# A cross network's last unit: second recursion level inside two products, one more addition on TensorE, and output blocks that leave by other queues and in halves

## The chip, the cores and the metric

The kernel runs on one core of a Trainium2 chip. The metric is device time in microseconds (us), the median of a few executions on one chip, lower is better. The experiments ran on several chips, each beside the kernel before on the same chip; its median in those rounds was 2277.26 to 2277.31 us. The profile is one execution; its span is some 2 us shorter than the time of the same execution. All runs quoted as timed were in the undisturbed state, with a granted TensorE clock of 0.998 to 1.0. The one exception is a run that was looked at once only, whose state is unknown; it is named where it comes up.

Most times below are counted from the first product matmul of the last unit, which I call **F**. "Tail" means F to the end of the span. A "run" is an experiment; where a store is said to have 512 "runs", these are its contiguous pieces in memory.

## The reference, cut to what matters

```python
B, D, L = 16384, 1024, 6            # bf16
x = x0
for l in range(L):
    proj = x @ ws[l] + bs[l]
    x = x0 * proj + x
return x
```

## The kernel before

The batch is cut in 16 blocks of 1024 rows; each goes through 6 layers, which makes 96 **units**. A unit is one 1024 x 1024 x 1024 product by Strassen-Winograd: seven half-size products P1 to P7 instead of eight. In most units products 5 and 2 are split the same way a second time: 56 matmuls of 256 columns in place of 32 of 512. x is kept transposed (features on partitions), so the last unit must turn its result round before it is stored.

Every operation has a rank, and operations are put into the engines' programs in rank order as their inputs are ready. The last unit has ranks of its own (`RLAST`). It is single-level here, as all units of the first row block are:

```python
units = [(pr, l) for pr in range(NPAIR) for l in range(L)]
NU = len(units)
level1 = lambda u: units[u][0] == 0 or u == NU - 1
...
        for m in range(KH):
            group(f"P1.{m}", "1", pA[m], A[m], B11, [XI[0, 0]], m, True)
            if one:                       # 16 matmuls of 512 columns for each of P2 and P5
                copy(f"F1.{m}", pX[m][:], pA[m][:], [A[m]], [Xn[m]])
                group(f"P2.{m}", "2", pX[m], Xn[m], B21, [XI[1, 0], Xn[m]], m, False)
                biased(f"E2.{m}", Q[:, m, :], pX[m][:], 0, m, [Xn[m]], [f"Q.{m}"])
                group(f"P5.{m}", "5", pX[m], Xn[m], T[1], ["T1"], m, True)
                copy(f"E5.{m}", P5s[:, m, :], pX[m][:], [Xn[m]], [f"5c.{m}"])
            ...                           # else: seven inner products, 28 matmuls of 256 each
```

The output has four blocks: Q ("11"), U ("12"), V ("22") and W ("21"). Q and U are turned by a DMA transpose and then stored; V and W are turned by TensorE into PSUM (the accumulator memory), copied out as bf16 ("cast"), and stored. W's residual x is added by TensorE (`xW`, x transposed into the same bank); V's by VectorE (`Vx`).

```python
            for h in range(2):
                sl = slice(h * KQ, (h + 1) * KQ)
                for nm, C, q in (("U", U, (0, 1)), ("V", V, (1, 1))):
                    ...                                            # Ua, Um, Va, Vm: add P5, times x0
                ttop(f"Vx{h}", V[:, sl], V[:, sl], blk(xs, 1, 1)[:, sl], ADD, ...)
                ttop(f"Ux{h}", ...)
            for m in range(KH):
                ttop(f"Wm{m}", W[:, m, :], W[:, m, :], blk(x0T, 1, 0)[:, m, :], MULT, ...)
            for nm, n in (("Q", 0), ("U", 1)):
                def tr(n=n, xfin=xfin, xo=xo):
                    nc.sync.dma_start_transpose(out=xo[:, 0, n]..., in_=xfin[:, 0, n]...)
                add("tr" + nm, tr, ...)
                def st(n=n, xo=xo, r0=r0):
                    nc.sync.dma_start(out[r0 + n * NB:r0 + (n + 1) * NB, 0:H]..., xo[:, 0, n]...)
                add("st" + nm, st, [f"xo{nm}"], ["out"])
            ...                                                    # tV, xW, tW, casts, stVa, stVb, stWa, stWb
```

By rank SyncE's program is: transpose Q, transpose U, store Q, store U, then V's two halves and W's first; W's second half goes by ScalarE's queue.

Of the kernel before, what the change touches and what calls it, by code (L numbers as in the profile page):

```python
# [9 lines left out]
ADD = mybir.AluOpType.add  # L10
SUB = mybir.AluOpType.subtract
MULT = mybir.AluOpType.mult
# [5 lines left out]
def ranks(text):  # L18

    return {w.split("@")[0]: float(w.split("@")[1]) for w in text.split()}  # L20
# [106 lines left out]
T1@-1.18 5t13@.65 5t2@3.13 2t13@3.47 5t4@5.20 2t2@6.67 T2@7.01 2t4@8.14 T3@8.48 T4@9.61 2cc@12.46 Q1@13.20 Qm@14.47  # L127
5cc@15.61 Qa@16.21 Ua@17.45 Um@18.72 Ux@19.99 Va@21.12 Wma@23.49 Wmb@24.69 Wx@25.43 Vm@27.50 Vx@28.97
""")]
RLAST = {**R0, **ranks("""  # L130
P6.0@10.4 P6.1@11.3 P6.2@12.1 P6.3@13 P3.0@13.9 P3.1@14.7 P3.2@15.6 P3.3@16.4 P7.0@17.3 P7.1@18.2 P7.2@19 P7.3@19.9
P4.0@20.8 P4.1@21.6 P4.2@22.5 P4.3@23.3
P2.0@3.5 P2.1@4.4 P2.2@5.2 P2.3@6.1 P5.0@6.9 P5.1@7.8 P5.2@8.7 P5.3@9.5 tV.0@24.4 tV.1@24.6 tV.2@24.8 tV.3@25
xW.0@25.1 tW.0@25.2 xW.1@25.3 tW.1@25.4 xW.2@25.5 tW.2@25.6 xW.3@25.7 tW.3@26.6
F1.0@2.8 F1.1@3.2 F1.2@3.7 F1.3@4.1 E2.0@4.6 E2.1@5.4 E2.2@6.3 E2.3@7.2 E5.0@8.3 E5.1@9.2 E5.2@10 E5.3@10.9 F.0@11.5 F.1@12.3 F.2@13.2 F.3@14.1 E3.0@15 E3.1@15.8 E3.2@16.7 E3.3@17.5 E7.0@18.4 E7.1@19.3 E7.2@20.1 E7.3@21
E4.0@21.9 E4.1@22.7 E4.2@23.6 E4.3@24.4 cV.0@25 cV.1@25.1 cV.2@25.2 cV.3@25.3 cW.3@27
T4@12 Qm@12.5 Qa@13.6
Ua0@16.6 Um0@17.2 Ux0@17.8 Ua1@18.4 Um1@19 Ux1@19.6 Va0@20.4 Vm0@21 Vx0@21.3 Va1@21.6 Vm1@22.2 Vx1@22.8
Wm0@22.9 Wm1@23.7 Wm2@24.6 Wm3@25.4 cW.0@26.3 cW.1@26.5 cW.2@26.7
trQ@19 stQ@24 trU@22.5 stU@26 stVa@27 stVb@27.5 stWa@28 stWb@29  # L140
""")}
SPAN2, SPAN0 = 23.4, 24.2

# [2 lines left out]
def kernel(  # L146
# [7 lines left out]
    nc = tc.nc  # L154
    P = nc.NUM_PARTITIONS
    B, D = x0.shape
    L = ws.shape[0]
    KD = D // P
    KH = KD // 2
    H = D // 2  # L160
    NB = 512
# [3 lines left out]
    KQ, HQ, NQ = KH // 2, H // 2, NB // 2  # L165
# [12 lines left out]
    pA = [psum.tile([P, NB], FP32, name=f"pA{i}") for i in range(KH)]  # L178
    pX = [psum.tile([P, NB], FP32, name=f"pX{i}") for i in range(KH)]
    x0Ts = [work.tile([P, 2, KD, NB], BF16, name=f"x0T{i}") for i in range(2)]  # L180
    xsts = [work.tile([P, 2, KD, NB], BF16, name=f"xst{i}") for i in range(2)]
# [4 lines left out]
    P1s, P5s, Q, U, V, W = (work.tile([P, KH, NB], BF16, name=f"ev{i}") for i in range(6))  # L186
# [5 lines left out]
    b_all = const.tile([P, LK], FP32, name="b_all")  # L192

    def blk(t, dh, n):
        return t[:, n, dh * KH:(dh + 1) * KH, :]
# [12 lines left out]

    units = [(pr, l) for pr in range(NPAIR) for l in range(L)]
    NU = len(units)  # L210
    level1 = lambda u: units[u][0] == 0 or u == NU - 1
    RAW = [("4", "load"), ("w12", "stage"), ("1", "load"), ("2", "load")]
    MAKE = [(w, "make") for w in ("5", "6", "7", "3")]
    ring_seq = [(0, w, k) for w, k in RAW]
    for u, (pr, l) in enumerate(units):
        if pr == 0:
            ring_seq += [(u + 1, w, k) for w, k in RAW if l < L - 1] + [(u, w, k) for w, k in MAKE]
        else:
            order = "1 2 5 6 7 3 4" if level1(u) else "1 5 5i 2 2i 6 3 7 4"
            ring_seq += [(u, w, "load") for w in order.split()]  # L220
    wt, uses_left, live = {}, {}, []
    pos = {"next": 0}

# [43 lines left out]
    for u, (pr, l) in enumerate(units):  # L267
# [8 lines left out]
        def add(name, fn, rd=(), wr=(), weights=(), rk=rk, base=base, u=u):  # L276
            op(base + rk[name], fn, rd, wr, [(u, w) for w in weights])

        def ttop(name, o, a, b, o_, rd, wr, **kw):
            add(name, lambda: tt(o, a, b, o_), rd, wr, **kw)  # L280
# [11 lines left out]
        def biased(name, dst, src, eh, m, rd, wr, l=l):  # L292
            c = l * KD + eh * KH + m
            add(name, lambda: nc.scalar.activation(out=dst, in_=src, func=IDENT, bias=b_all[:, c:c + 1], scale=1.0), rd, wr)  # L294
# [114 lines left out]
                     ip5[X][:].unsqueeze(1).to_broadcast([P, 2, KQ, NQ]), ADD, [X + "u0", X + "u1", X + "ps"],  # L409
                     cn(0, 1) + cn(1, 1))  # L410
        for m in range(KH):
            xb = m if one else m % 2
            group(f"P6.{m}", "6", pA[m], A[m], T[2], ["T2", A[m]], m, False)
            copy(f"F.{m}", pX[xb][:], pA[m][:], [A[m]], [Xn[xb]])
            group(f"P3.{m}", "3", pX[xb], Xn[xb], B22, [XI[1, 1], Xn[xb]], m, False)
            biased(f"E3.{m}", U[:, m, :], pX[xb][:], 0, m, [Xn[xb]], [f"U.{m}"])
            group(f"P7.{m}", "7", pA[m], A[m], T[3], ["T3", A[m]], m, False)
            biased(f"E7.{m}", V[:, m, :], pA[m][:], 1, m, [A[m]], [f"V.{m}"])
            group(f"P4.{m}", "4", pA[m], A[m], T[4], ["T4", A[m]], m, False)
            biased(f"E4.{m}", W[:, m, :], pA[m][:], 1, m, [A[m]], [f"W.{m}"])  # L420
        allm = lambda s: [f"{s}.{m}" for m in range(KH)]
        if not one:
            ttop("Q1", Q[:], Q[:], P1s[:], ADD, allm("Q") + allm("P1s"), allm("Q"))
# [11 lines left out]
        else:  # L435
# [2 lines left out]
            quad = lambda t: t[:].rearrange("r n k (j p) -> r (n k j) p", p=P).rearrange(  # L438
                "r (e n j k) p -> r e n j k p", e=2, n=2, j=KH)
            xfin, xo = quad(xsts[free]), quad(x0Ts[free])  # L440
            XF = [f"xs.{free}.{a}{b}" for a, b in QD]
            XT = [f"x0.{free}.{a}{b}" for a, b in QD]
            r0 = pr * PR
# [5 lines left out]
# [3 lines that stand above are left out]
                    ms = half(nm, h)  # L452
                    ttop(f"{nm}a{h}", C[:, sl], C[:, sl], P5s[:, sl], ADD, ms + half("5c", h), ms)
                    ttop(f"{nm}m{h}", C[:, sl], C[:, sl], blk(x0T, *q)[:, sl], MULT, ms + [X0[q]], ms)
                ttop(f"Vx{h}", V[:, sl], V[:, sl], blk(xs, 1, 1)[:, sl], ADD, half("V", h) + [XI[1, 1]], half("V", h))
                ttop(f"Ux{h}", xfin[:, 0, 1].rearrange("r j k p -> r k j p")[:, sl], v4(U[:])[:, sl],
                     v4(blk(xs, 0, 1))[:, sl], ADD, half("U", h) + [XI[0, 1]] + XF, [f"xfU{h}"])
            for m in range(KH):
                ttop(f"Wm{m}", W[:, m, :], W[:, m, :], blk(x0T, 1, 0)[:, m, :], MULT, [f"W.{m}", X0[1, 0]], [f"W.{m}"])
            for nm, n in (("Q", 0), ("U", 1)):  # L460
                def tr(n=n, xfin=xfin, xo=xo):
                    nc.sync.dma_start_transpose(out=xo[:, 0, n].rearrange("p j k r -> p (j k) r"),
                                                in_=xfin[:, 0, n].rearrange("r j k p -> r (j k p)"))
                add("tr" + nm, tr, [f"xf{nm}0", f"xf{nm}1"] + XT, [f"xo{nm}"])

                def st(n=n, xo=xo, r0=r0):
                    nc.sync.dma_start(out[r0 + n * NB:r0 + (n + 1) * NB, 0:H].rearrange("(j p) d -> p j d", p=P),
                                      xo[:, 0, n].rearrange("p j k r -> p j (k r)"))
                add("st" + nm, st, [f"xo{nm}"], ["out"])
            for nm, C, bank, n in (("V", V, pX, 1), ("W", W, pA, 0)):  # L470
                for m in range(KH):
                    bn = (Xn if nm == "V" else A)[m]

                    def part(src, start, stop, bank=bank, m=m):
                        for j in range(KH):
                            nc.tensor.matmul(bank[m][:, j * P:(j + 1) * P], lhsT=src[:, m, j * P:(j + 1) * P], rhs=ident[:],
                                             start=(start and j == 0), stop=stop, skip_group_check=True)
                    if nm == "W":
                        add(f"xW.{m}", lambda part=part, xs=xs: part(blk(xs, 1, 0), True, False), [XI[1, 0]], [bn])
                    add(f"t{nm}.{m}", lambda part=part, C=C, nm=nm: part(C, nm == "V", True), [f"{nm}.{m}", bn], [bn])  # L480

                    def cp(bank=bank, m=m, n=n, nm=nm, xo=xo):
                        d, s_ = xo[:, 1, n][:, :, m, :], bank[m][:].rearrange("p (j r) -> p j r", r=P)
                        if nm == "V" or m == 3:
                            nc.scalar.copy(out=d, in_=s_)
                        else:
                            nc.vector.tensor_copy(out=d, in_=s_)  # L487
                    add(f"c{nm}.{m}", cp, [bn] + XT, [f"xo{nm}.{m}"])

                def st2(k0, k1, eng=nc.sync, n=n, xo=xo, r0=r0):  # L490
                    eng.dma_start(out[r0 + n * NB:r0 + (n + 1) * NB, H + k0 * P:H + k1 * P].rearrange("(j p) d -> p j d", p=P),
                                      xo[:, 1, n][:, :, k0:k1].rearrange("p j k r -> p j (k r)"))
                add(f"st{nm}a", lambda st2=st2: st2(0, KQ), half(f"xo{nm}", 0), ["out"])
                add(f"st{nm}b", lambda st2=st2, nm=nm: st2(KQ, KH, nc.sync if nm == "V" else nc.scalar), half(f"xo{nm}", 1), ["out"])
# [118 lines left out]
```

## Time and profile before

| what | value | from |
|---|---|---|
| time | 2277.72 us | median of three runs (2276.81 to 2277.87) |
| span of the profiled execution, clock | 2275.2 us, 0.999 | profile |
| F to the end of product 4 on TensorE | 24.17 us | timeline of TensorE |
| F to the end of the last cast | 27.91 us | timelines of VectorE and ScalarE |
| F to the last landing of a store | 31.75 us | landings in the trace |
| F to the end of the span (tail) | 33.07 us | 2275.24 - 2242.17 |

The lines of the profile are shown in the prediction. The tail has two chains: compute (up to the last cast at 27.91) and the 16 shared DMA engines (full for the 9.5 us from 21.8 to 31.3).

### The profile page before, as it was taken

The numbers are of one execution on the slowest core, as the hardware profiler recorded it, in microseconds if no ns is written. First come the engines' busy times: TensorE is split into PE (matmuls) and PEld (weight loads), VectorE is DVE, ScalarE is ACT, GpSimd is POOL, SyncE is SP. The second block draws the span as 40 slices with busy tenths as digits, with TensorE's granted clock in tenths as the row PEclk, the third lists the DMA queues.
The fourth block names the chain that finished last, engine by engine and source line by source line (L and its number), as shares of the span: only waits on it lengthen the run. The fifth ranks groups of instructions, "written<-read, shape, count | busy, mean of one in ns | idle before, by whom it ended". The sixth has DMA issues, their size and how long they took to land.

```text
span 2275.2 us, 34978 instructions
## 1 busy us (share of the span) xinstructions
PE 2265.4 (100%) x12951; PEld 1264.0 (56%) x12951; DVE 2079.9 (91%) x2326; ACT 1839.4 (81%) x3228; POOL 22.1 (1%) x43
## 2 busy tenths in 40 slices
PE   9999999999999999999999999999999999999998
PEld 4455555555555555555555555555555555555554
DVE  7999999999999999999999999999999999999997
ACT  5678888888888888888888888888888888888887
POOL 1110000000000000000000000000000000000000
PEclk9999999999999999999999999999999999999999
DMA  9779797796977969779697796978969689696872
GB/s 279 229 270 289 261 242 269 219 301 209 252 257 221 288 217 260 250 226 283 213 274 241 228 283 204 273 245 230 283 200 292 226 232 286 194 303 216 241 240 65
DMA packets 625868, 557.01 MB, mean 245 GB/s; under 512 B 397600, under 2 KB 552224, under 8 KB 625696
## 3 DMA queue, kind: packets, MB, share of 16 engines
q1 hardware_dynamic: 618864, 534.58, 79.1%
q0 software_dynamic: 5184, 18.88, 2.2%
q8 instruction: 101, 1.65, 0.3%
q10 hardware_dynamic: 1648, 1.32, 0.2%
q14 instruction: 71, 0.58, 0.1%
HBM read 436.22 MB, written 52.43 MB: 215 GB/s over the span
## 4 chain that ended last, share of the span: by engine, by line
PE 98%; DVE 1%; SPq 0%; DMA 0%; issue 0%; ACT 0%; DVEq 0%
PE pA L285 57%; PE pX L389 24%; PE pX L285 16%; DVE ev L198 1%; SPq L529 0%; DMA wp<-in_ws_dram 0%; DVE xst L198 0%; DVE T L198 0%; DVE ti L198 0%; DVE wp L198 0%; SPq L538 0%; ACT ev L294 0%; DVE x0T L487 0%; DVEq L608 0%; DVEq L198 0%
## 5 line engine op out<-in xcount | busy, mean ns | idle before, releaser
L285 PEld LDWEIGHTS <-wp 128*128 128x128 bf16 x7904 | 772.3, 98 | 843.7 <-issue 3.9
L285 PE MATMUL pA<-T,wp 128*128 128x512 bf16 x4608 | 1054.9, 379 | 0.5 <-DVE T L198 0.5
L294 ACT ACTIVATE ev<-pA,b_all 128x512 bf16<-128x512 f32 x1124 | 704.8, 690 | 211.8 <-PE pA L285 211.4
L389 PEld LDWEIGHTS <-wp 128*128 128x128 bf16 x4984 | 487.1, 98 | 156.6 <-issue 15.2
L198 DVE TENSOR_TENSOR ev<-ev,x0T 128x2048 bf16<-128x2048 bf16 (+2 forms) x484 | 482.7, 999 | 8.1 <-ACT ev L294 1.5
L198 DVE TENSOR_TENSOR xst<-ev,xst 128x2048 bf16<-128x2048 bf16 x319 | 388.9, 1219 | 18.6 <-DVE ev L198 0.5
L389 PE MATMUL pX<-ti,wp 128*128 128x256 bf16 x2848 | 397.6, 272 | 0.0
L198 DVE TENSOR_TENSOR ev<-ev,ev 128x2048 bf16<-128x2048 bf16 (+1 forms) x283 | 343.7, 1215 | 26.7 <-ACT ev L294 9.8
L294 ACT ACTIVATE ev<-pX,b_all 128x512 bf16<-128x512 f32 x412 | 289.4, 705 | 59.9 <-PE pX L285 49.3
L285 PE MATMUL pX<-xst,wp 128*128 128x512 bf16 x1376 | 336.4, 379 | 0.0
L285 PE MATMUL pA<-xst,wp 128*128 128x512 bf16 x1280 | 313.5, 379 | 0.0
L290 ACT COPY pX<-pA 128x512 f32<-128x512 f32 x412 | 256.3, 625 | 44.7 <-PE pA L285 44.3
L290 ACT CAST ev<-pX 128x512 bf16<-128x512 f32 x384 | 224.8, 619 | 49.0 <-ACT ev L294 37.6
L198 DVE TENSOR_TENSOR ev<-iu,ip 128x1024 bf16<-128x1024 bf16 x178 | 122.4, 688 | 120.7 <-ACT iu L290 120.7
L290 ACT COPY pX<-pX 128x512 f32<-128x512 f32 x356 | 208.7, 587 | 8.4
L290 ACT CAST iu<-pX 128x512 bf16<-128x512 f32 x356 | 196.8, 639 | 0.0
L198 DVE TENSOR_TENSOR T<-xst 128x2048 bf16<-128x2048 bf16 x160 | 194.8, 1217 | 0.3
L198 DVE TENSOR_TENSOR T<-xst,T 128x2048 bf16<-128x2048 bf16 x160 | 194.5, 1216 | 0.0
L389 PE MATMUL pX<-T,wp 128*128 128x256 bf16 x1068 | 160.2, 273 | 0.0
L290 ACT CAST ip<-pX 128x512 bf16<-128x512 f32 x178 | 104.7, 589 | 54.1 <-PE pX L389 54.1
L389 PE MATMUL pX<-xst,wp 128*128 128x256 bf16 x888 | 133.2, 273 | 0.0
L198 DVE TENSOR_TENSOR xst<-ev,x0T 128x2048 bf16<-128x2048 bf16 x64 | 78.2, 1222 | 1.6
(44 smaller groups left out, 624.3 us busy)
## 6 DMA issues: line engine op xcount, KB each, us to landing
wp<-Lc SPq DMA_DIRECT2D x538, 512.0 KB, 4.6
wp<-in_ws_dram SPq DMA_DIRECT2D x285, 512.0 KB, 5.3
out_dram<-x0T SPq DMA_DIRECT2D x30, 1024.0 KB, 8.6
Lc<-wp POOLq DMA_DIRECT2D x24, 512.0 KB, 6.2
Lc<-isum POOLq DMA_DIRECT2D x12, 512.0 KB, 6.9
w<-in_ws_dram SPq DMA_DIRECT2D x5, 512.0 KB, 6.3
wp<-in_ws_dram ACTq DMA_DIRECT2D x2, 512.0 KB, 5.8
out_dram<-x0T SPq DMA_DIRECT2D x2, 512.0 KB, 3.6
```

Of the source, the lines that this page charges most:

```text
L198: nc.vector.tensor_tensor(out=o, in0=a, in1=b, op=op)
L285: nc.tensor.matmul(bank[:], lhsT=wt[(u, w)][:, k, m * P:(m + 1) * P], rhs=rhs[:, k, :], start=(start and k == 0), stop=(k == KH - 1), skip ...
L290: add(name, lambda: nc.scalar.copy(out=dst, in_=src), rd, wr)
L294: add(name, lambda: nc.scalar.activation(out=dst, in_=src, func=IDENT, bias=b_all[:, c:c + 1], scale=1.0), rd, wr)
L389: nc.tensor.matmul(pX[bank][:, m * NQ:(m + 1) * NQ], lhsT=wv[:, k, m * P:(m + 1) * P], rhs=rhs[:, k, :], start=(start and m == 0 and k == ...
```

## The change

Its intent is to save TensorE 0.74 us by the second level, to take work from VectorE (the addition of x to V, and one bias-add that is fused with a multiply), and to let Q and U leave before V and W need the DMA engines. The core of the diff (the new ranks, and access patterns, are cut):

```diff
-level1 = lambda u: units[u][0] == 0 or u == NU - 1
+level1 = lambda u: units[u][0] == 0
...
-                biased(f"E4.{m}", W[:, m, :], pA[m][:], 1, m, [A[m]], [f"W.{m}"])
+            if not (last and m == KH - 1):
+                biased(f"E4.{m}", W[:, m, :], pA[m][:], 1, m, [A[m]], [f"W.{m}"])
...
-                ttop(f"Vx{h}", V[:, sl], V[:, sl], blk(xs, 1, 1)[:, sl], ADD, ...)
...
-            for m in range(KH):
+            for m in range(KH - 1):
                 ttop(f"Wm{m}", ...)
+            add("Wm3", lambda c=c, x0T=x0T: nc.vector.scalar_tensor_tensor(
+                out=W[:, KH - 1, :], in0=pA[KH - 1][:], scalar=b_all[:, c:c + 1],
+                in1=blk(x0T, 1, 0)[:, KH - 1, :], op0=ADD, op1=MULT), ...)
+            outs = [("Q", xfin[:, 0, 0], xo[:, 0, 0], 0, 0, H)]
+            outs += [(f"U{h}", xfU[:, h], xoU[:, h], NB, h * HQ, (h + 1) * HQ) for h in range(2)]
+            for nm, src, dst, r, c0, c1 in outs:
+                add("tr" + nm, lambda src=src, dst=dst: nc.sync.dma_start_transpose(...), ...)
+                add("st" + nm, lambda ...: nc.gpsimd.dma_start(out[r:r + NB, c0:c1]..., dst...), ...)
...
-                    if nm == "W":
-                        add(f"xW.{m}", ...)
+                    add(f"x{nm}.{m}", lambda part=part, xs=xs, n=n: part(blk(xs, 1, n), True, False), [XI[1, n]], [bn])
...
-                        if nm == "V" or m == 3:
+                        if nm == "V" or m in (0, 2):      # which casts ScalarE does
```

More of the change, by code (lines that the diff above doesn't have):

```diff
@@ L129 @@
 """)]
-RLAST = {**R0, **ranks("""
-P6.0@10.4 P6.1@11.3 P6.2@12.1 P6.3@13 P3.0@13.9 P3.1@14.7 P3.2@15.6 P3.3@16.4 P7.0@17.3 P7.1@18.2 P7.2@19 P7.3@19.9
-P4.0@20.8 P4.1@21.6 P4.2@22.5 P4.3@23.3
-P2.0@3.5 P2.1@4.4 P2.2@5.2 P2.3@6.1 P5.0@6.9 P5.1@7.8 P5.2@8.7 P5.3@9.5 tV.0@24.4 tV.1@24.6 tV.2@24.8 tV.3@25
-xW.0@25.1 tW.0@25.2 xW.1@25.3 tW.1@25.4 xW.2@25.5 tW.2@25.6 xW.3@25.7 tW.3@26.6
-F1.0@2.8 F1.1@3.2 F1.2@3.7 F1.3@4.1 E2.0@4.6 E2.1@5.4 E2.2@6.3 E2.3@7.2 E5.0@8.3 E5.1@9.2 E5.2@10 E5.3@10.9 F.0@11.5 F.1@12.3 F.2@13.2 F.3@14.1 E3.0@15 E3.1@15.8 E3.2@16.7 E3.3@17.5 E7.0@18.4 E7.1@19.3 E7.2@20.1 E7.3@21
-E4.0@21.9 E4.1@22.7 E4.2@23.6 E4.3@24.4 cV.0@25 cV.1@25.1 cV.2@25.2 cV.3@25.3 cW.3@27
-T4@12 Qm@12.5 Qa@13.6
-Ua0@16.6 Um0@17.2 Ux0@17.8 Ua1@18.4 Um1@19 Ux1@19.6 Va0@20.4 Vm0@21 Vx0@21.3 Va1@21.6 Vm1@22.2 Vx1@22.8
-Wm0@22.9 Wm1@23.7 Wm2@24.6 Wm3@25.4 cW.0@26.3 cW.1@26.5 cW.2@26.7
-trQ@19 stQ@24 trU@22.5 stU@26 stVa@27 stVb@27.5 stWa@28 stWb@29
+RLAST = {**R2, **ranks("""
+xV.0@24.3 tV.0@24.4 xV.1@24.5 tV.1@24.6 xV.2@24.7 tV.2@24.8 xV.3@24.9 tV.3@25 xW.0@25.1 tW.0@25.2 xW.1@25.3 tW.1@25.4 xW.2@25.5 tW.2@25.6 xW.3@25.7 tW.3@26.6
+P7.0@16.48 P7.1@17.34 P4.0@19.93 P4.1@20.8 E7.0@18.41 E7.1@18.98 E4.0@21.87 E4.1@22.44
+cV.0@25 cV.1@25.1 cV.2@25.2 cV.3@25.3 cW.3@27
+Q1@13 Qm@14 Qa@15
+Ua0@16 Um0@16.6 Ux0@17.2 Ua1@17.8 Um1@18.4 Ux1@19 Va0@19.8 Vm0@20.4 Vx0@20.7 Va1@21 Vm1@21.6 Vx1@22.2
+Wm0@22.4 Wm1@23.2 Wm2@24.1 Wm3@25 cW.0@26.3 cW.1@26.5 cW.2@26.7
+trQ@17 stQ@18 trU0@18.5 trU1@20 stU0@24 stU1@26 stVa@27 stVb@27.5 stWa@28 stWb@29
 """)}
@@ L218 @@
         else:
-            order = "1 2 5 6 7 3 4" if level1(u) else "1 5 5i 2 2i 6 3 7 4"
-            ring_seq += [(u, w, "load") for w in order.split()]
+            ring_seq += [(u, w, "load") for w in "1 5 5i 2 2i 6 3 7 4".split()]
     wt, uses_left, live = {}, {}, []
@@ L411 @@
         for m in range(KH):
-            xb = m if one else m % 2
+            xb = m if one or last else m % 2
             group(f"P6.{m}", "6", pA[m], A[m], T[2], ["T2", A[m]], m, False)
@@ L440 @@
             xfin, xo = quad(xsts[free]), quad(x0Ts[free])
+            halves = lambda t: t[:].rearrange("r n k (j p) -> r (n k j) p", p=P)[:, KH * KH:2 * KH * KH].rearrange(
+                "r (h j k) p -> r h j k p", h=2, j=KH)
+            xfU, xoU = halves(xsts[free]), halves(x0Ts[free])
             XF = [f"xs.{free}.{a}{b}" for a, b in QD]
@@ L454 @@
                     ttop(f"{nm}m{h}", C[:, sl], C[:, sl], blk(x0T, *q)[:, sl], MULT, ms + [X0[q]], ms)
-                ttop(f"Vx{h}", V[:, sl], V[:, sl], blk(xs, 1, 1)[:, sl], ADD, half("V", h) + [XI[1, 1]], half("V", h))
-                ttop(f"Ux{h}", xfin[:, 0, 1].rearrange("r j k p -> r k j p")[:, sl], v4(U[:])[:, sl],
+                ttop(f"Ux{h}", xfU[:, h].rearrange("r j k p -> r k j p"), v4(U[:])[:, sl],
                      v4(blk(xs, 0, 1))[:, sl], ADD, half("U", h) + [XI[0, 1]] + XF, [f"xfU{h}"])
-            for m in range(KH):
+            for m in range(KH - 1):
@@ L459 @@
                 ttop(f"Wm{m}", W[:, m, :], W[:, m, :], blk(x0T, 1, 0)[:, m, :], MULT, [f"W.{m}", X0[1, 0]], [f"W.{m}"])
-            for nm, n in (("Q", 0), ("U", 1)):
-                def tr(n=n, xfin=xfin, xo=xo):
-                    nc.sync.dma_start_transpose(out=xo[:, 0, n].rearrange("p j k r -> p (j k) r"),
-                                                in_=xfin[:, 0, n].rearrange("r j k p -> r (j k p)"))
-                add("tr" + nm, tr, [f"xf{nm}0", f"xf{nm}1"] + XT, [f"xo{nm}"])
-                def st(n=n, xo=xo, r0=r0):
-                    nc.sync.dma_start(out[r0 + n * NB:r0 + (n + 1) * NB, 0:H].rearrange("(j p) d -> p j d", p=P),
-                                      xo[:, 0, n].rearrange("p j k r -> p j (k r)"))
-                add("st" + nm, st, [f"xo{nm}"], ["out"])
+            c = l * KD + 2 * KH - 1
@@ new lines @@
+            add("Wm3", lambda c=c, x0T=x0T: nc.vector.scalar_tensor_tensor(
+                out=W[:, KH - 1, :], in0=pA[KH - 1][:], scalar=b_all[:, c:c + 1], in1=blk(x0T, 1, 0)[:, KH - 1, :], op0=ADD, op1=MULT),
+                [A[KH - 1], X0[1, 0]], [f"W.{KH - 1}"])
+            outs = [("Q", xfin[:, 0, 0], xo[:, 0, 0], 0, 0, H)]
+            outs += [(f"U{h}", xfU[:, h], xoU[:, h], NB, h * HQ, (h + 1) * HQ) for h in range(2)]
+            for nm, src, dst, r, c0, c1 in outs:
+                add("tr" + nm, lambda src=src, dst=dst: nc.sync.dma_start_transpose(
+                    out=dst.rearrange("p j k r -> p (j k) r"), in_=src.rearrange("r j k p -> r (j k p)")),
+                    (["xfQ0", "xfQ1"] if nm == "Q" else ["xf" + nm]) + XT, ["xo" + nm])
+                add("st" + nm, lambda dst=dst, r=r0 + r, c0=c0, c1=c1: nc.gpsimd.dma_start(
+                    out[r:r + NB, c0:c1].rearrange("(j p) d -> p j d", p=P), dst.rearrange("p j k r -> p j (k r)")),
+                    ["xo" + nm], ["out"])
@@ L477, in part @@
                                              start=(start and j == 0), stop=stop, skip_group_check=True)
-                    if nm == "W":
-                        add(f"xW.{m}", lambda part=part, xs=xs: part(blk(xs, 1, 0), True, False), [XI[1, 0]], [bn])
-                    add(f"t{nm}.{m}", lambda part=part, C=C, nm=nm: part(C, nm == "V", True), [f"{nm}.{m}", bn], [bn])
+                    add(f"x{nm}.{m}", lambda part=part, xs=xs, n=n: part(blk(xs, 1, n), True, False), [XI[1, n]], [bn])
+                    add(f"t{nm}.{m}", lambda part=part, C=C: part(C, False, True), [f"{nm}.{m}", bn], [bn])
                     def cp(bank=bank, m=m, n=n, nm=nm, xo=xo):
                         d, s_ = xo[:, 1, n][:, :, m, :], bank[m][:].rearrange("p (j r) -> p j r", r=P)
-                        if nm == "V" or m == 3:
+                        if nm == "V" or m in (0, 2):
                             nc.scalar.copy(out=d, in_=s_)
```

## The prediction

> **What bounds the kernel now.** I read the page first, for the engine that sets the end.
>
> ```profile
> PE 2265.4 (100%) x12951; PEld 1264.0 (56%) x12951; DVE 2079.9 (91%) x2326; ACT 1839.4 (81%) x3228; POOL 22.1 (1%) x43
> PE 98%; DVE 1%; SPq 0%; DMA 0%; issue 0%; ACT 0%; DVEq 0%
> ```
>
> TensorE is on 98% of the chain that ended last, so its instruction count sets the time. But there are 96 units (16 row blocks, 6 layers) and the change touches only the last one. What is at stake is one unit and the tail after it, some 33 us of 2275. So next I read the busy times over the last two units. The window edges are the starts of their first matmul, read from TensorE's timeline.
>
> ```profile
> 2218.73:2242.17 23.44, 23.44 (x137) 13.31 (x136) 20.68 (x25) 19.28 (x35) 0.00 (x0) 1.00 0.08 23
> 2242.17:2266.35 24.18, 24.18 (x114) 10.96 (x113) 19.09 (x23) 18.08 (x29) 0.00 (x0) 1.00 0.22 43
> ```
>
> The unit before the last already has the second level in products 5 and 2, and takes 23.44 us of TensorE without a gap. The last has one level only and takes 24.18. Then the chain of waits in the final stretch:
>
> ```profile
> 2257.91 0.70 ACT ev L294
> 2258.61 0.02 issue
> 2258.63 0.70 DVE ev L198
> ...
> 2266.25 1.08 DVE ev L198 x3
> 2267.33 0.20 issue
> 2267.53 0.75 DVE ev L198 x2
> 2268.28 1.20 DVE x0T L487 x2
> 2269.48 0.60 DVEq L608
> ```
>
> From 2258.6 to 2270.1 VectorE is on the chain, not TensorE: twelve half-block operations on U and V, four on W, three casts out of PSUM. After 2270.1 only transfers are left. The timelines of SyncE and ScalarE show how they are issued:
>
> ```profile
> 2254.48 9.70 SPq L462 DMA_TRANSPOSE x0T<-xst  x2
> 2264.28 3.33 SPq L467 DMA_DIRECT2D out_dram<-x0T  x2
> 2268.22 1.96 SPq L491 DMA_DIRECT2D out_dram<-x0T  x3
> 2270.16 0.39 ACTq L491 DMA_DIRECT2D out_dram<-x0T  x1
> ```
>
> Block Q was transposed from 2254.5 and landed at 2258.9, but its store was queued behind U's transpose and went out at 2264.28 (one half megabyte waits 5.3 us for nothing). The busy times by stretch (last two columns: DMA share, GB/s) show what that costs:
>
> ```profile
> 2258.00:2264.00 6.00, 6.00 (x30) 2.69 (x29) 5.20 (x8) 4.77 (x8) 0.00 (x0) 1.00 0.04 8
> 2264.00:2266.50 2.50, 2.50 (x15) 1.19 (x14) 2.40 (x5) 2.02 (x3) 0.00 (x0) 1.00 1.08 205
> 2266.50:2268.00 1.50, 1.46 (x27) 1.29 (x25) 1.50 (x5) 1.45 (x3) 0.00 (x0) 1.00 1.04 349
> 2268.00:2270.00 2.00, 1.41 (x26) 1.23 (x23) 2.00 (x4) 1.73 (x4) 0.00 (x0) 1.00 0.92 304
> 2270.00:2273.00 3.00, 0.00 (x0) 0.00 (x0) 0.08 (x1) 0.03 (x1) 0.00 (x0) 0.75 0.96 284
> ```
>
> The DMA engines idle for 6 us, then are full from 2264.0 to 2273.5. **Two things bound the end side by side**: compute until 2270.1 plus one transfer, and 9.5 us of transfer work that cannot start before 2264. The last landing is at 2273.9; the span closes 1.3 us later.
>
> **What the Trainium skill says.** (1) "TensorE: Matmul & The Clock Gate", "Wait — 56ns, not 53.3ns?": matmuls start N/2.4 GHz plus about 2.5 ns apart. The trace agrees: 216 ns at 512 columns, 109 at 256, 55.6 at 128. (2) "DMA: Bandwidth & Descriptors", "Issuing engines are not separate DMA queues": transfers of all issuing engines share the same 16 DMA engines, so another queue saves issue time only. The rows above are already at 0.92 to 1.08 of all engines; the GpSimd queue cannot add bandwidth, only take Q's store out of SyncE's order. (3) Same page, "Latency and other measured facts": first byte after about 1 us from GpSimd, 0.6 us from SyncE. The early saves of weight sums on the GpSimd queue land in 3.0 us at best, SyncE's two 512 KB stores here in 3.0 and 4.3: no large penalty. (4) "SBUF — State Buffer", "Who interferes with whom": a VectorE operation with two SBUF inputs blocks GpSimd's reads, while descriptor generation needs the write side (inferred there). The early issues on GpSimd take 531 ns each beside a busy VectorE, so I expect no starvation; but they have 128 runs of 4 KB, and the new stores have 512 runs of 0.5 or 1 KB.
>
> **The change part by part.**
> 1. *Second level in products 5 and 2.* Removes 32 matmuls of 512 columns, adds 56 of 256: 32 x 0.216 = 6.91 against 56 x 0.109 = 6.12 us, minus 0.79. The two units above give minus 0.74 as run. TensorE's product 4 ends at 2265.61 instead of 2266.35. Two more 512 KB weight loads are issued over 20 us early: free.
> 2. *VectorE work this brings.* The inner sums (0.69 + 2 x 0.42 us for each of two products), two recombinations (0.69 each) and Q's add (1.23) land on VectorE before the tail. In the unit before, Q's last add ends at 2236.10; plus 23.44 gives 2259.54, against 2254.46 now. So U's first operation starts at about 2259.44, 0.8 later than the 2258.63 shown.
> 3. *VectorE work this removes.* Adding x to V by TensorE drops two half-block adds. U's six operations take 4.12 us as now (2258.63 to 2262.75); V's four take 2 x (0.72 + 0.61) = 2.66 instead of 4.11. W starts at 2259.44 + 4.12 + 2.66 = 2266.2, against 2266.86: 0.65 earlier. Three multiplies (0.34 apart) lead to 2267.2; the fused bias-and-multiply of W's last block reads PSUM, an estimated 0.7 like the casts (0.68), to 2267.9. It saves ScalarE's last eviction (0.69). Two casts instead of three: VectorE alone could finish at 2269.1.
> 4. *TensorE work this adds.* V's x costs 16 transposing matmuls of 55.6 ns, 0.89 us, and all 64 now follow product 4 without a wait: 2265.61 + 64 x 0.0556 = 2269.17. Before, the last transpose ended at about 2269.24, with 0.2 us of waits. **The 0.74 won is spent on the 0.89 added.** Result to semaphore took 0.23 us after the last start before, so the last cast starts at 2269.37 and, being on VectorE (0.68) instead of ScalarE (0.58), ends at 2270.05. Before: 2270.08. Compute gains about nothing.
> 5. *Q and U leave earlier.* Q's transpose is issued at 2259.6, data from about 2260.7 (before, 1.1 after issue). U's halves follow at 2261.6 and 2263.7. Transfer work from there: transposes 2 x 2.5, Q's store 1.5 (0.52 MB at 349 GB/s), U's 1.8 (its halves now have 512-byte runs, at the 284 GB/s of the last row), V and W 3.7. Sum 12.0: 2272.7 if nothing idles. I allow 0.4 for landings between transpose and store: data end at 2273.1, against 2273.5. From the other side, the last store is issued at 2270.1 and lands 3.0 (an unqueued one) to 3.8 us later (as now): 2273.1 to 2273.9. I put the last landing at 2273.4, 0.5 earlier than 2273.9.
>
> **Sum**: minus 0.5 us on the span; 2277.7 becomes 2277.2.
>
> **Rivals.**
> A. *TensorE's own shortening counts*: minus 0.7 to minus 1.0. For it: transfers are lighter at the end, since Q and U may be gone before V and W come, and ScalarE's casts of V start a microsecond earlier. Against it: the 16 added transposes, and the last store still waits for the last cast at 2270.05. It would make 2276.7 to 2277.0.
> B. *The GpSimd queue is slow*: 512 short runs per store may cost four times the 531 ns of 128 runs, 2.1 us each, three in a row from 2264.2, so U's second half goes out at 2270 and competes with V and W. Then data end near 2274, time 2277.7 to 2278.5. Against it: the early issues show no blocking, and short runs are not shown to cost more anywhere in this trace.
> C. *VectorE stays the bound*: if Q's add comes later than in the unit before, everything shifts one to one; a microsecond late gives plus 0.4. Against it: the unit before shows the same pattern running without gaps.
>
> **Range and chances.** The certain terms nearly cancel; the rest is how transfers interleave, minus 1.0 to plus 0.8. The three runs before spread over 1.1 us. Together: 2275.9 to 2278.4 should hold it 8 times in 10. 2% is 46 us, more than the whole touched stretch; only a disturbed run could show that.
>
> **What would show each step.** Product 4 ending 23.4 us after the unit's first matmul (step 1); Q's add ending 5.1 us later than before (2); W's first multiply near 2266.2 (3); 64 transposes back to back, last cast ending within 0.2 us of 2270.1 (4); Q's store before U's second transpose lands, and DMA share near 1 from about 2261 to 2273 (5). Wrong would be: GpSimd issues of well over 0.6 us each, a DMA pause between 2264 and 2268, or a TensorE gap before the transposes.

## The result and the profile after

The changed kernel took **2280.53 us** (four runs, 2279.53 to 2281.1); the kernel before, in the same rounds, 2277.26 (2276.79 to 2277.87). The ratio is 1.0014, with a 95% interval of 0.9996 to 1.0031. Ratios here are the mean time of one kernel's fast runs over the mean of the other's of the same rounds, so not quite the ratio of the medians. 2280.53 lies outside the predicted range of 2275.9 to 2278.4. Repeated in later rounds (run `e5_again`), it took 2279.53 against 2277.28.

How much of 3.3 us is real? In this profiled execution, F came 1.76 us later (2243.93 against 2242.17), although nothing before F's unit had been touched: a VectorE operation 40 us into the run was already 1.36 late. In the repeat F came at 2242.08, 0.09 *earlier* than before. So the late start is a chance of that execution and not the kernel's; the other three were not profiled, but the repeat's median, a microsecond lower, fits. What repeats is the tail: 35.39 and 35.42 us against 33.07, **2.3 us longer**, and that is what must be explained.

First the page of the changed kernel: engines' busy times, and shares of the chain that ended last.

```profile
PE 2255.2 (99%) x12753; PEld 1268.1 (56%) x12991; DVE 2084.0 (91%) x2332; ACT 1843.9 (81%) x3234; POOL 23.3 (1%) x46
PE 98%; issue 1%; DVE 1%; DMA 0%; ACT 0%; SPq 0%; DVEq 0%
```

At this scale nothing is to be seen, except that GpSimd has three instructions more, the stores. (TensorE's lower matmul count is no gain: some matmul records are missing from this trace; weight loads, 40 more, are complete.) The chain of waits in the final stretch:

```profile
2260.63 6.91 PE pA L281 x32
2267.54 1.79 PE pX L478 x32
2269.33 1.80 PE pA L478 x32
2271.13 0.02 issue
2271.15 0.69 DVE x0T L488
```

Products 7 and 4 run into the 64 transposing matmuls without a gap, then comes one cast. VectorE's twelve half-block operations, which led this chain before, are no longer on it. The last cast ends at 2271.84, which is F + 27.91, exactly as before. **The compute chain did what it was meant to do and its end did not move.** The rest of the tail is transfers. The busy times by stretch (us, then busy time and instructions of TensorE, its weight load, VectorE, ScalarE, GpSimd; granted clock; DMA share; GB/s):

```profile
2262.30:2268.30 6.00, 6.00 (x42) 3.18 (x40) 5.83 (x11) 4.40 (x7) 0.00 (x0) 1.00 0.99 176
2268.30:2270.00 1.70, 1.70 (x34) 1.70 (x32) 1.39 (x4) 1.70 (x5) 1.03 (x2) 1.00 0.03 10
2270.00:2274.00 4.00, 1.11 (x20) 0.94 (x17) 1.38 (x2) 1.15 (x3) 1.24 (x2) 0.94 0.99 286
2274.00:2277.50 3.50, 0.00 (x0) 0.00 (x0) 0.00 (x0) 0.00 (x0) 0.00 (x0) 0.50 0.91 271
```

Look at the column before the last. The DMA engines are full for 6 us with the three transposes, then **all but idle for 1.7 us** (0.03), then full again to the end. The timelines of GpSimd and SyncE say what was missing in the idle stretch (the bracket is the idle time before the operation and what ended it):

```profile
2268.97 2.27 POOL L469 DMA_DIRECT2D out_dram<-x0T  x3 [2104.81 <-issue]
```

```profile
2261.28 5.34 SPq L466 DMA_TRANSPOSE x0T<-xst  x3
2269.12 3.55 SPq L492 DMA_DIRECT2D out_dram<-x0T  x3
```

Q's transpose was issued at 2261.28 and landed, by the trace, at 2265.67; the last wait instruction before the store ended at 2266.16. GpSimd's store of Q began at 2268.97: 3.30 us after the landing, and **2.81 us after the last wait in front of it had ended**. It had rested for 2104.81 us, and "issue" as releaser means that the profile shows no cause. By then U's halves had landed too, so three stores went out in a burst, at the moment at which V's stores began on SyncE. Beside them the stores of V and W took longer. Their times from issue to landing, before (first) and after:

```profile
DMA to landing us min/median/max: 2.9/3.3/3.8
```

```profile
DMA to landing us min/median/max: 3.7/6.2/6.9
```

The last landing came 3.84 us after the last cast before, and 6.15 us after it now.

### The profile page after: what moved, and what is told of

Read it like the earlier page. It is cut to its first block, busy times and chain, and to the rows that moved or that the text cites. A ratio compares the mean times of both kernels' runs of the same rounds, so it can differ in the third digit from the quotient of the medians.

```text
span 2279.3 us, 34840 instructions
## 1 busy us (share of the span) xinstructions
PE 2255.2 (99%) x12753; PEld 1268.1 (56%) x12991; DVE 2084.0 (91%) x2332; ACT 1843.9 (81%) x3234; POOL 23.3 (1%) x46
## 4 chain that ended last, share of the span: by engine, by line
PE 98%; issue 1%; DVE 1%; DMA 0%; ACT 0%; SPq 0%; DVEq 0%
PE pA L281 57%; PE pX L385 24%; PE pX L281 16%; DMA x0T<-in_x_dram 0%; DVE ev L195 0%; DVE xst L195 0%; DVE T L195 0%; DVE ti L195 0%; PE pA L478 0%; PE pX L478 0%; SPq L530 0%; ACT ev L290 0%; DVE x0T L488 0%; ACT pX L286 0%; DVEq L195 0%
## 5 line engine op out<-in xcount | busy, mean ns | idle before, releaser
L281 PE MATMUL pA<-xst,wp 128*128 128x512 bf16 x1204 | 302.5, 379 | 4.0
```

What stands on the lines that cost most here:

```text
L281: nc.tensor.matmul(bank[:], lhsT=wt[(u, w)][:, k, m * P:(m + 1) * P], rhs=rhs[:, k, :], start=(start and k == 0), stop=(k == KH - 1), skip ...
```

## The experiments

The quantity compared is the tail, because a median of four runs scatters by half a microsecond to one, as large as the effects. Each tail is that of one profiled execution; the changed kernel's two are 0.03 apart. The differences of the medians from the kernel before agree with those of the tails within 0.3 us, but for the first result with its late start. The table has all runs; times are from F. "Before" in the last column is the kernel before in the same rounds.

| run | product 4 ends | last cast ends | last landing | tail | median, before |
|---|---|---|---|---|---|
| kernel before | 24.17 | 27.91 | 31.75 | 33.07 | 2277.26 |
| changed kernel | 23.44 | 27.91 | 34.05 | 35.39 | 2280.53, 2277.26 |
| `e1_warm` | 23.44 | 27.91 | 32.67 | 33.99 | 2278.12, 2277.27 |
| `e2_sync` | 23.44 | 27.91 | 32.99 | 34.15 | 2278.18, 2277.27 |
| `e3_level_only` | 23.44 | 28.67 | 32.45 | 33.65 | 2278.14, 2277.27 |
| `e4_stores_only` | 24.17 | 27.90 | 32.10 | 33.06 | 2277.08, 2277.27 |
| `e5_again` | 23.44 | 27.90 | 34.15 | 35.42 | 2279.53, 2277.28 |
| `e6_q_gone` | 23.44 | 27.91 | 31.85 | 33.20 | 2277.12, 2277.28 |
| `e7_early_q` | 24.17 | 27.91 | 31.20 | 32.40 | 2276.89, 2277.28 |
| `e8_rests` (one run) | 23.44 | 27.90 | 32.60 | 33.89 | 2277.89, 2277.28 |
| `e9_shift` | 23.44 | 27.90 | 32.56 | 33.89 | 2277.94, 2277.31 |
| `e10_old_stores` | 23.44 | 27.90 | 33.07 | 34.33 | 2278.74, 2277.31 |
| `e11_stores_shift` | 24.17 | 27.90 | 31.19 | 32.11 | 2276.21, 2277.31 |

**Theory T**: GpSimd's first store after its long rest starts late. **Rival R1**: VectorE's operations block GpSimd. The Trainium skill, "SBUF — State Buffer", section "Who interferes with whom", says that VectorE operations with two SBUF inputs contend with GpSimd instructions that read SBUF (a store's issue is not shown to be one), and VectorE is busy with such operations just then. **Rival R2**: crowding; Q, now 5 us later, meets U, V and W on the DMA engines, and the queue doesn't matter.

### Run 1: a tiny transfer on GpSimd's queue ten microseconds earlier

```diff
+            warm = dram.tile([P, 16], BF16, name="warm")
+            add("warm", lambda warm=warm: nc.gpsimd.dma_start(warm[:], P5s[:, 0, NQ:NQ + 16]), ["5c.0"], [])
```

> Tail = from the first product matmul of the last unit to the end of the span: 33.0 us before, 35.4 changed. In the changed kernel Q's store on the GpSimd queue started at 2269.0, 2.8 us after its last wait was met. This run sends one tiny transfer on the same queue some 10 us earlier. Theory cold (the queue's first transfer after 2.1 ms of rest starts late): Q's store starts within 0.5 us of the landing of its transpose (plus 0.3 for its waits), tail 33.0 to 33.6. Theory VectorE (a stream of two-input operations keeps GpSimd out until it ends): the start stays about 3 us late, tail about 35.4.

GpSimd's timeline in this run:

```profile
2254.44 0.54 POOL L473 DMA_DIRECT2D warm<-ev  x1 [2091.75 <-DVE ev L195]
2264.86 0.76 POOL L469 DMA_DIRECT2D out_dram<-x0T  x1 [9.87 <-DMA x0T<-xst]
2266.01 0.76 POOL L469 DMA_DIRECT2D out_dram<-x0T  x1 [0.39 <-issue]
2267.47 0.75 POOL L469 DMA_DIRECT2D out_dram<-x0T  x1 [0.70 <-DMA x0T<-xst]
```

Q's store now starts 0.7 us after its transpose's landing, and its releaser is named again. The tail falls from 35.39 to 33.99. VectorE's operations in the stretch are those of the changed kernel, so **R1 falls**. But the tiny transfer itself started 0.28 us after its release, after 2.09 ms of rest: the long rest alone isn't the cause either. And 33.99 is still 0.92 above 33.07: something is left for R2.

### Run 2: the changed kernel with these stores on SyncE

```diff
-trQ@17 stQ@18 trU0@18.5 trU1@20 ...
+trQ@17 trU0@18.5 stQ@19 trU1@20 ...
-                add("st" + nm, lambda ...: nc.gpsimd.dma_start(
+                add("st" + nm, lambda ...: nc.sync.dma_start(
```

> All of the change, but the stores of blocks 11 and 12 on SyncE's queue, in the order transpose Q, transpose U half 0, store Q, transpose U half 1, stores of U. If the late start on the GpSimd queue is the whole loss: the pause of the transfers between 2268 and 2270 is gone and the tail is 33.0 to 33.6. If halving U (512-byte runs) or the traffic itself is the loss: tail stays above 34.5.

34.15, 0.55 above what I had expected at most. In SyncE's program U's second transpose stands behind Q's store; it was issued at F + 22.27 (21.45 in the changed kernel), and V's stores and W's first followed late in turn: W's first half was issued at 28.97, against 27.55. A queue in program order with nine issues has its own price. The run therefore says nothing against T, and shows that the expectation left out SyncE's order.

### Run 3: the second level alone

```diff
# on the kernel before, with ranks of the changed kernel
-    level1 = lambda u: units[u][0] == 0 or u == NU - 1
+    level1 = lambda u: units[u][0] == 0
-            xb = m if one else m % 2
+            xb = m if one or last else m % 2
```

> The kernel before plus the second level alone (old stores, old V). TensorE's product 4 ends 0.7 us earlier (23.44 after the first matmul instead of 24.18). VectorE carries more in front and still adds x to V: W's multiplies and casts end 0.8 later than before. Theory VectorE bound: last cast 28.7 us after the first matmul, tail 33.6 to 34.0. Rival, TensorE bound: tail 32.3.

Product 4 ends at 23.44, and the last cast at 28.67: VectorE, with Q's add 5 us later and all its old work, ends 0.76 later. The tail is 33.65. So the second level by itself makes the tail 0.6 us **longer**; the additions to TensorE and the fused operation buy the 0.76 of compute back.

### Run 4: the new stores alone

The kernel before with U in halves and the stores of Q and U on GpSimd's queue; single level, so that Q is ready 5 us earlier.

```diff
-trQ@19 stQ@24 trU@22.5 stU@26 ...
+trQ@13.7 stQ@14 trU0@18.5 trU1@20 stU0@24 stU1@26 ...
+            outs = [("Q", ...)] + [(f"U{h}", ...) for h in range(2)]
+                add("tr" + nm, lambda ...: nc.sync.dma_start_transpose(...), ...)
+                add("st" + nm, lambda ...: nc.gpsimd.dma_start(...), ...)
```

> The kernel before plus the halves and the GpSimd queue alone. Q's store may start 3 us late as well, but Q is ready at 2258.9, so it is gone before U: no pause matters. Theory late start: last cast unchanged (27.9 us after the first matmul), last landing 0.4 to 0.9 earlier, tail 32.1 to 32.7. Rival (the GpSimd queue or the halves cost transfer time as such): tail 34 or more.

33.06, no gain at all, a miss. (The last landing is even 0.35 us later than before, 32.10 against 31.75; but from there to the end of the span it takes 0.96 us here, and 0.92 in run 11, against 1.16 to 1.35 in all other runs. Nothing here explains this.) GpSimd's timeline begins with

```profile
2261.57 0.76 POOL L469 DMA_DIRECT2D out_dram<-x0T  x1 [2099.22 <-issue]
```

while the wait for Q's landing had ended at 2258.77: late by 2.80 us, almost the same amount as 2.81 in the changed kernel, at another time and beside other work. Q's store then ran into U's second transpose, which landed at 25.09 (in run 11, where Q's store is prompt, the same transpose landed at 23.79).

### Run 5: the changed kernel again

> The changed kernel once more. The tail (first product matmul of the last unit to the end) explains 2.3 us of the 3.3 us by which the medians differ; the profiled run also began its first layers 1.4 us late, though nothing there was changed. Theory chance: start within 0.5 us of the kernel before, Q's store again 2.8 us after its waits, tail 35.2 to 35.5, median 2.0 to 2.6 above before. Rival (the start belongs to the kernel): start again over 1 us late, median over 3 above.

Tail 35.42, and the store of Q starts 2.88 us after its last wait and 3.39 after the landing. The late start repeats, the late F does not.

### Run 6: the changed kernel without Q's transfers at the end

Wrong result (relative error 0.177): run 1, with Q's transpose dropped and its store, with old contents, ranked at the unit's start. The trace shows it issued at 2140.76 already, 102 us before F; either way it is gone before the end.

```diff
-warm@12 trQ@17 stQ@18 ...
+warm@12 trQ@17 stQ@1 ...
+                if nm != "Q":
                   add("tr" + nm, ...)
```

> Wrong result on purpose: as e1_warm, but Q is not transposed and its store sends old contents at the start of the last unit. e1_warm kept a tail of 34.0 with the late start removed, and the second level makes Q 5 us later than before, into the crowded end. Theory crowding (Q's 2.7 us of transpose and 1.7 us of store in the last 13 us are the rest): tail 32.3 to 33.0. Rival (packets of the GpSimd queue or U's halves hold up V and W): tail 33.6 or more.

33.20, against 33.99 in run 1. So Q's traffic in the last 13 us costs 0.79 of the remaining 0.92. **R2 holds for this part.** The 0.13 that is left is not proof that nothing else costs: the kernel before, with which 33.20 is compared, has Q's store in its own full stretch (issued at 25.06, landed at 28.07). Against run 7 below, which has no traffic of Q there either, run 6's last landing is still 0.65 later (31.85 and 31.20). U's transposes are issued 0.8 us later in it (19.40 and 21.45, against 18.63 and 20.69) and V's stores 0.86 earlier (25.19 against 26.05), so more meets at once; that this is the reason was not tested.

### Run 7: Q's store early, on SyncE

```diff
# on run 4
-trQ@13.7 stQ@14 trU0@18.5 trU1@20 stU0@24 stU1@26 ...
+trQ@13.7 stQ@14 trU0@18.5 trU1@20 stU0@21 stU1@24 ...
-   nc.gpsimd.dma_start(
+   nc.sync.dma_start(
```

> The kernel before, with Q's store right behind its own transpose and U in halves, all on SyncE; one level in the last unit, V as before. Q then leaves while the transfers rest. Theory crowding: only U's last half, V and W are left at the end; last cast 27.9 after the first matmul, last landing 31.1 to 31.4 instead of 31.75, tail 32.3 to 32.8, 0.3 to 0.7 us faster than before. Rival (V and W alone fill the end, e4's result): tail 33.0 to 33.2.

32.40, 0.67 less than before: Q's store is issued at 16.77, the moment its transpose lands, and is gone at 19.78, before U's halves are turned. It is the first run whose tail is clearly below that of the kernel before. Its time is 2276.89 against 2277.28, ratio 0.9998 (0.9986 to 1.0011), not separable by the timed runs alone.

### Runs 8 and 9: what is the late start?

Three theories are left after run 1: the rest (something runs down in 2.1 ms); the first use of a store of this form; or the fetch of GpSimd's instructions. The last one came from the trace. The changed kernel's DMA queues between the wait and the store (2266.2 to 2269; packets, MB, share):

```profile
q1 hardware_dynamic: 1113, 0.27, 64.8%
q14 instruction: 1, 0.01, 0.7%
```

One 8 KB packet of the instruction queue q14 falls in this wait, at 2267.3: 1.1 us after the waits are met and 1.7 before the store starts. In runs 4 and 5 it is the same, at 2259.8 and 2265.5. In run 1 no such packet is there. (This queue is not GpSimd's alone: the kernel before, whose GpSimd does nothing then, has 65 of its packets from 200 us on. That the one in question is GpSimd's is inferred from its time.)

Run 8 puts tiny GpSimd transfers into four earlier units, so that rests of 81 to 562 us precede one transfer each, and one of 1041 us Q's store. Run 9 keeps the full rest and only moves GpSimd's instruction stream, by eight tiny memsets at the kernel's very start:

```diff
# run 8, on the changed kernel
+        if u in (10, 16, 28, 52):
+            op(base + 12, lambda dm=dm, u=u: nc.gpsimd.dma_start(dm[:], wt[(u, "4")][:, 0, 0:16]), [], [], [(u, "4")])
# run 9, on the changed kernel
+    pad = const.tile([P, 8], BF16, name="pad")
+    for i in range(8):
+        nc.gpsimd.memset(pad[:, i:i + 1], 0.0)
```

> The changed kernel plus four tiny GpSimd-queue transfers after rests of some 90, 140, 280 and 560 us, each behind a separate wait for a weight load, as Q's store is behind its wait. Measured: start of each after the landing it waits for, and Q's store after some 1000 us. Theory rest: short rests start within 0.5 us, long ones near 2.8 late, Q's store late as well. Theory first use of the form (512 runs): the four start promptly whatever the rest, Q's store 2.8 late. Theory end of kernel: same as the second.

> The changed kernel with eight tiny GpSimd memsets at the very start, 2.2 ms before the stores: nothing near the end differs, and the queue rests as long (from some 162 us to the end). In the three late runs one 8 KB packet on an instruction queue appears 1.0 to 1.3 us after the waits are met and 1.7 us before the transfer starts; in the prompt ones none. Theory instruction fetch (the store's instruction lay in a block not yet fetched): the memsets move that edge, Q's store starts 0.5 to 0.7 us after its transpose lands, no such packet, tail 33.8 to 34.2. Theory rest (2.1 ms without a transfer makes the queue slow): start 3.3 us after the landing, tail 35.4.

In run 8 the four tiny transfers start 0.89, 0.52, 0.52 and 0.52 us after the landing they wait for, whatever the rest, and Q's store 0.69. In run 9 GpSimd's timeline is

```profile
2264.55 0.76 POOL L469 DMA_DIRECT2D out_dram<-x0T  x1 [2101.82 <-DMA x0T<-xst]
2265.81 0.77 POOL L469 DMA_DIRECT2D out_dram<-x0T  x1 [0.49 <-issue]
2267.24 0.75 POOL L469 DMA_DIRECT2D out_dram<-x0T  x1 [0.67 <-DMA x0T<-xst]
```

2101.82 us of rest, nothing of this form before it, and the store starts 0.68 us after the landing. **Rest and form fall.** The instruction packets of the last 45 us (window 2230 to 2275), changed kernel first, run 9 second:

```profile
q14 instruction: 3, 0.02, 0.2%
```

```profile
q14 instruction: 2, 0.02, 0.1%
```

In run 9 the additional packet is at 151.8 us instead, where GpSimd is still at its early work. The other traces can be read for the same packet. All thirteen have 71 packets of 8 KB on q14 from the kernel's start on, 70 of them at about the same places, and one moves: to about 175 us where GpSimd issues no store at the end (the kernel before, runs 2, 3, 7 and 10), to 165.9 in run 1 and 247 in run 8 (just behind the first tiny transfer), to 151.8 and 151.5 in runs 9 and 11, and into the wait in the changed kernel and in runs 4 and 5. In run 6, where Q's dummy store comes before the tiny transfer in GpSimd's program, the packet is at 2138.9, between the end of that store's last wait (2135.18) and its start (2140.76): late once more, by 5.58 us. So run 1 may have helped by its place in GpSimd's program, not because it warmed a queue. The late start comes with an instruction packet that falls into the wait, and goes when the program is shifted. Run 9's DMA engines between first transpose and last data:

```profile
2260.60:2274.40 13.80, 8.70 (x88) 5.81 (x86) 8.48 (x15) 7.24 (x12) 2.28 (x3) 0.99 0.92 229
```

13.8 us at 0.92 is 12.7 us of full engines. The tail is 33.89: the late start was worth 1.5 us.

### Run 10: the changed compute with the old stores

```diff
# on the changed kernel: the transposes and stores of Q and U as before, on SyncE
-trQ@17 stQ@18 trU0@18.5 trU1@20 stU0@24 stU1@26 ...
+trQ@17 trU@20 stQ@24 stU@26 ...
```

> The changed kernel with the way out of Q and U as before: whole U, SyncE, Q's store behind U's transpose. Last cast as in the change, 27.9 us after the first matmul. Theory crowding (Q 5 us later alone fills the end): Q and U transposed from 17.4 to 25.7, stores after that; tail 33.3 to 34.0, between before (33.07) and the change (35.4). Rival (what delays the change is only its halves and its queue): tail 33.0 or less.

34.33, 0.33 above the range. With Q late, the old order of stores is worse than the new one on a prompt GpSimd queue (33.89), by 0.44 us.

### Run 11: the kernel before with the new stores and a shifted GpSimd program

```diff
# on run 4
+    pad = const.tile([P, 8], BF16, name="pad")
+    for i in range(8):
+        nc.gpsimd.memset(pad[:, i:i + 1], 0.0)
```

> e4_stores_only (one level, halves, GpSimd queue) plus the same eight memsets. Theory instruction fetch: Q's store starts within 0.7 us of the landing of its transpose instead of 2.8, U's halves are not held up behind it, tail 32.3 to 32.8 as in e7_early_q, instead of 33.06. Rival (the GpSimd queue itself holds V and W up): tail stays at 33.0.

```profile
2259.50 0.77 POOL L469 DMA_DIRECT2D out_dram<-x0T  x1 [2097.00 <-DMA x0T<-xst]
2264.84 0.77 POOL L469 DMA_DIRECT2D out_dram<-x0T  x1 [4.58 <-issue]
2266.59 0.75 POOL L469 DMA_DIRECT2D out_dram<-x0T  x1 [0.98 <-DMA x0T<-xst]
```

The same shift, put on another kernel, again makes the first store prompt. The tail is **32.11**, 0.95 below run 4, which differs only by the eight memsets, and 0.96 below the kernel before. The time is 2276.21 (five runs, 2275.55 to 2277.05) against 2277.31; the ratio is 0.9996 (0.9982 to 1.0009), so the timed runs alone do not prove a gain of this size, and the tail is what shows it. Of the 0.96, only 0.56 is an earlier last landing (31.19 against 31.75); the other 0.40 is the shorter stretch after it, noted at run 4. The last landing is that of run 7 (31.20). These two, single level and Q away early, are the best versions.

## Why the prediction was wrong

Going through its own steps, with F taken out:

1. **Second level, minus 0.74: right.** Product 4 ends at 23.44 instead of 24.17.
2. **Q's add 5.1 us later: right.** It ends at F + 17.33 (2261.26), against 12.29 before: 5.04. 
3. **VectorE's work: right.** The fused operation took 0.74 (estimated 0.7) and started at F + 25.02, as predicted for the end of W's third multiply:

```profile
2267.33 1.70 DVE L195 TENSOR_TENSOR ev<-ev,x0T 128x1024 bf16<-128x1024 bf16 x4
2268.95 0.74 DVE L460 SCALAR_TENSOR_TENSOR ev<-pA,b_all,x0T 128x512 bf16<-128x512 f32 x1
```

4. **64 transposes back to back, compute gain about nothing: right.** 1.79 + 1.80 us of them; the last cast ends at 27.91 from F in both kernels.
5. **The transfers: this step failed.** It put the last landing at 2273.4, which is F + 31.2; it came at 34.05. Two terms of it were wrong.
   - *"I allow 0.4 for landings between transpose and store"*, with Q's store issued as its transpose lands. The store started 2.81 us after the waits were met, and the engines stood idle for 1.7 us on end. Removing that by run 1 or run 9 gives back 1.4 or 1.5 us of the tail. The prediction had named "a DMA pause between 2264 and 2268" as a sign of being wrong, and this is it (2266.5 to 2268.2, with F taken out), but not for the cause that it had in mind.
   - *"Sum 12.0"*, and again the 0.4, now with a prompt queue. The sum reckoned transfers at the rates they have alone and in order. Run 9 has 12.7 us of full engines, and from its first packet (F + 18.54) to its last (F + 32.21) about 1.0 us of idle time: 0.7 more work and 0.6 more idle time than predicted. So data end at F + 32.2; predicted were 18.5 + 12.4 = 30.9. The mechanism, Q's transpose inside the full stretch, was in the sum; its size was not enough.

The tail's 2.32 us, as run: 1.40 late start (35.39 - 33.99), 0.79 Q's traffic in the full stretch (33.99 - 33.20), 0.13 balance (33.20 - 33.07), in which a gain from Q's absence and a cost that was not tracked down stand against each other (run 6). The step's heading, "Q and U leave earlier", is what misled: Q's store was to leave earlier, but Q's transpose was issued at F + 12.31 before, on idle engines, and at 17.35 now, at the head of a full stretch. To be ready later and stored earlier leaves no slack for any delay between the two.

Of the rivals, A (a shorter TensorE program shows in full) fell: the compute chain ends where it did. B (GpSimd's queue is slow) had the right place and the wrong mechanism: it reckoned 2.1 us for each issue of 512 runs, and the issues take 0.75 to 0.77. Its outcome, 2277.7 to 2278.5, is what runs 1 and 9 show (2278.12 and 2277.94) once the late start is gone, but by luck: the reason is another. C (VectorE as the bound) is what run 3 shows for the second level alone, not for the whole change.

**What stays open.** Which rule decides when GpSimd's next block of instructions is fetched, and why the fetch waits until the semaphores are met rather than running during 2.1 ms of rest, is not settled. The runs show that the packet and the late start come and go together, in four late runs (the changed kernel, 4, 5, and the first store of 6) and four prompt ones (1, 8, 9, 11), and that moving the program moves both; that the packet is the fetch for which the store waits is the reading that fits, not a thing that the trace states. Nor is it shown how far the unequal packets (4096 bytes for the stores on GpSimd's queue, 512 for those of V and W) slowed V and W; run 2, without GpSimd, had W land at 32.99 all the same.

## What to carry to other kernels

At the end of a kernel, ask first when each block's *transfer* can start: here the second level saved TensorE 0.74 us but finished one block 5 us later, and this block's transfers then cost 0.79 us where the DMA engines were full. Where one engine's queue has been at rest and gets a store on the critical path, look in the trace for an instruction packet in its wait; a few instructions more in front of it moved the packet away here (runs 9 and 11), which is worth a try, but has to be checked again after every edit of that engine's program. Compare tails from a common event, not only medians: the start of a run varied by over a microsecond here, as much as half the effect.

## What the Trainium skill lacked or had wrong

- "Runtime: NRT & Kernel Launch", section "Instruction fetch mechanics", says that instructions are streamed in 16 KiB blocks by the sequencer's own queue and that crossing a block's boundary is mostly hidden. Here, if the packet is such a block, it was not hidden: GpSimd's store started 2.80 to 2.88 us after its last wait in three runs (5.58 in a fourth), with one instruction packet in between, and promptly when the program was shifted (0.68 us after the landing). The packets seen here are 8 KB (71 packets, 0.58 MB in a run).
- "DMA: Bandwidth & Descriptors", section "Latency and other measured facts", gives about 1 us to the first byte for GpSimd's queue and 0.6 us for SyncE's. Here the first data packet came later: on engines that were idle, 1.34 us after the start of GpSimd's issue (run 11) and 0.93 us after SyncE's (run 7), both for Q's store. No page gives a number for what an issue on GpSimd costs by its number of runs: 0.531 us for 128 runs, 0.75 to 0.77 for 512.
- The same page, section "Queues, rings and completion order", says that a DMA engine takes turns between queues packet by packet. It doesn't say what that means for queues with unequal packets. In the changed kernel, with 4096-byte packets on one queue and 512-byte packets on the other, V's second store took 6.9 us to land (2.9 before); the share of the packet size in that was not isolated.
- "SBUF — State Buffer", section "Who interferes with whom", had led me to consider VectorE as what holds GpSimd's stores back, though it infers that descriptor generation is not held back by such operations. The runs bear the inference out: beside the same VectorE operations with two SBUF inputs, Q's store started 0.7 us after its landing in runs 1 and 9.
